# Moving work between engines in the first scan of a fused SSD and GELU kernel

## The chip, the cores and the metric

The kernel runs on one core of one Trainium2 chip. The time is device time in microseconds (us) of one launch, given as the median of several runs. All arithmetic on matrices is in fp32; in the records a fp32 matmul appears as two records.

## What is computed

Two layers, one behind the other. The first is a state space scan in chunks over 4 batches, 8 heads and 768 positions, with head width 32 and state width 16:

```python
L = np.exp(cum[:, :, :, None] - cum[:, :, None, :]) * causal
CB = np.einsum('bhin,bhjn->bhij', Cc, Bc)
y_intra = np.einsum('bhij,bhjd->bhid', CB * L, xc)
y_inter = np.einsum('bhin,bhnd->bhid', Cc, state) * np.exp(cum)[:, :, :, None]
y[:, :, sl] = y_intra + y_inter
state = decay_full * state + np.sum(Bx, axis=2)
```

`cum` is the running sum of `log(a)` inside a chunk. The result, 3072 tokens by 256, goes through a feed-forward layer with 2048 hidden columns:

```python
h = x @ w_in
g = h * (1.0 / (1.0 + np.exp(-1.702 * h)))
out = g @ w_out
```

The weights and the output differ in type: the weights come as float64 and are unpacked on the chip into fp32.

## The kernel before

The 3072 tokens are worked on in six groups of 512 (`NG = 6`, `TG = 512`). A group is two pairs of 128-token chunks (`PG = 2`). Scan chunks are 64 positions long (`H = 64`), so that a group holds eight of them. For each group the scan yields `yT`, its transposed output, and the feed-forward layer then computes 16 blocks `h` of 128 hidden columns each and the products with `w_out`. Groups 0 and 1 do the start of the feed-forward layer with plain matmuls (`hidden`, L889); group 0's products are plain too (`project_all`, L987); the rest uses a scheme with seven products (`first`, L945 and L955; `product`, L1050 and L1057).

The order of the work on each engine is the order in which the code issues it, and it is fixed at the end (`in_order`): no scheduler changes it. Each engine works through its own queue; waits between engines are semaphores that follow from the tiles. SyncE's queue issues nearly all transfers, in order too.

The change touches the first scan, group 0, both pairs p = 0 and 1, which is written out by hand in L1165 to L1212. Its steps:

- `keep_busy` and `pads` (L435, L428): matmuls on ones whose result nobody uses. `pads(9, busy)` at L1171 stands ahead of the last of eight masks (`mask`, L548), which lay -1e5 above the diagonal into PSUM.
- `turn_first` (L612): VectorE transposes C and B in 32x32 blocks as soon as they have landed.
- `differ_of` (L1153, matmuls L554) and `decay_exp` (L570, ScalarE L575): the decay matrix L = exp(difference of `cum`) for both pairs.
- `mask_first` (L644): C for each pair is spread into two copies `CT`, one for each of the Q = 2 heads that share 32 partitions, each multiplied by the column `part[:, q]`, which is 1 on that head's rows and 0 elsewhere. GpSimd does both pairs (L650). For pair 1 a one-element memset by VectorE (L649) holds it back.
- `fields` (L188): VectorE splits the upper words of a piece of weights into exponent and mantissa (L192, L195). `clamp` (L198, ScalarE L203, L204), `rounded` (L206, VectorE L208) and `join` (L215, VectorE L222 and L228) make fp32 of it. Piece i of `PIECES` holds some of the 16 column blocks: piece 0 blocks 0 and 1, piece 1 blocks 2 and 3, piece 2 blocks 4 and 5.
- `turn_back` (L622, L627): TensorE transposes B back. `ends_first` (L465, VectorE L468): B times the decay to the end of the chunk, `Be`.
- `score` (L669, matmuls L682): the products of C and B. Both pairs' results lie in one tile of PSUM. Between the two pairs `since_first` is called (L506): two matmuls of rows (L512) and two exponentials by ScalarE (L517) that give `since`, the decay since the start of a chunk.
- `weigh` (L688, VectorE L693): L times the scores, pair by pair. `fetch(1, held=True)` (L163) writes one element by VectorE (L171) between the two; the transfer of piece 1, and all transfers behind it on SyncE's queue, wait for it.
- `drops` (L520): ScalarE spreads the decay of each chunk over 64 columns for the scan (L522, 448 elements in each partition).
- `gain` (L701, matmuls L713): the increments of the state, `A`, in two banks. `parts_first` (L726, L730): ScalarE copies them into `steps`, so that the eight chunks of a column lie side by side.
- `since_start` (L661, L667), on GpSimd here: `CsT`, C times `since`.
- `keep_first` (L732): one VectorE scan over `drop` and `steps` (L735) gives the states of all eight chunks. The states are then copied for each pair into `state[p]`, half of each by ScalarE (L743) and half by VectorE (L744), each half multiplied by its column of `part`.
- `dense(2)` (L1157, L1161): two further matmuls of ones.
- `finish` (L788): on TensorE the parts inside the chunks (`intra`, L833), then the parts from the states (`inter`, L821), and ScalarE's copies into `yT` (L850). Then `hidden(0, f)` begins.

`hidden(1, f)` splits its first matmuls by columns: the first two (f = 0) in four pieces of 128 columns, the next three in two pieces of 256.

## Time and profile before

| | us |
|---|---|
| three runs | 350.84, 352.07, 352.6 |
| median | 352.07 |
| the profiled execution | 349.68 |
| its span, first to last instruction | 347.8 |
| TensorE busy in the span | 342.0 (98%) |
| VectorE busy | 253.5 (73%) |
| ScalarE busy | 153.1 (44%) |
| GpSimd busy | 12.9 (4%) |

The granted TensorE clock is 1.000 over the span. A profile lists instructions with the line of the code that issued them, the tile that they write and the tiles that they read. In a timeline a row gives the start, the time from the start of the first to the end of the last instruction of the row, engine, line, operation, operands, shapes and count; in square brackets stands idle time of that engine ahead of it and what ended it ("issue" where the profile shows nothing that was waited for). PE is TensorE, PEld its weight loads, DVE VectorE, ACT ScalarE, POOL GpSimd, and SPq SyncE's queue of transfers. Instructions of one engine overlap by some hundredths of a microsecond, and a matmul's end is modelled, so starts are compared with starts.

### The profile page before, as it was taken

Reading aid. Unit: us, or ns where it says so; the run is one execution under the profiler, and the core shown is the slowest. Engines: PE = TensorE matmul, PEld = TensorE weight load, DVE = VectorE, ACT = ScalarE, POOL = GpSimd, SP = SyncE. Lnnn points to the kernel's source line nnn. Section 1 sums busy time; section 2 is a strip of 40 time slices with the busy share of each in tenths; the row PEclk is TensorE's granted clock in tenths of the full one; section 3 lists DMA queues with packets and bytes.
Section 4 is the critical chain, followed back from the end, with each engine's and each line's share of the span. In section 5 each row is a group of like instructions: output and inputs, shape, how many; then the busy total and the mean of one; then the engine's idle time right before and its main releaser. Section 6 shows DMA issues by size and latency. Waiting matters only on the chain.

```text
span 347.8 us, 8141 instructions
## 1 busy us (share of the span) xinstructions
PE 342.0 (98%) x3392; PEld 271.9 (78%) x3392; DVE 253.5 (73%) x479; ACT 153.1 (44%) x349; POOL 12.9 (4%) x41
## 2 busy tenths in 40 slices
PE   8899999999999999999999999999999999999996
PEld 6644444557788888888888888888888888899996
DVE  5899999998679998839995649787555654455463
ACT  5698573107354324744332543442444321554320
POOL 8300000000000100000000000000000000000000
PEclk9999999999999999999999999999999999999999
DMA  6699997435526100435613036300000300000301
GB/s 162 142 336 193 283 212 155 81 77 93 105 58 128 33 2 15 63 104 102 101 28 50 2 81 117 64 2 1 2 2 2 61 2 0 0 2 0 62 0 61
DMA packets 89980, 25.92 MB, mean 75 GB/s; under 512 B 73432, under 2 KB 87128, under 8 KB 89944
## 3 DMA queue, kind: packets, MB, share of 16 engines
q1 hardware_dynamic: 89112, 24.88, 33.3%
q10 hardware_dynamic: 832, 0.52, 0.5%
q8 instruction: 26, 0.43, 0.5%
q14 instruction: 10, 0.08, 0.1%
HBM read 22.15 MB, written 3.24 MB: 73 GB/s over the span
## 4 chain that ended last, share of the span: by engine, by line
PE 97%; ACT 1%; DVE 1%; issue 0%; DVEq 0%
PE acc L1050 28%; PE X L945 20%; PE Y L955 14%; PE h L889 10%; PE o L987 8%; PE acc L1057 7%; PE y L833 2%; PE y L821 2%; PE cb L682 2%; PE A L713 1%; PE busy L440 1%; PE ab L554 1%; PE ab L548 0%; DVE steps L735 0%; ACT steps L730 0%; ACT drop L522 0%
## 5 line engine op out<-in xcount | busy, mean ns | idle before, releaser
L950 ACT ACTIVATE ac<-X 128x256 f32<-128x256 f32 x76 | 29.1, 383 | 78.6 <-PE X L945 78.2
L1050 PE MATMUL acc<-mg,mw 128*128 128x256 f32 x192 | 54.5, 379 | 0.0
L922 ACT ACTIVATE gT<-gT 128x512 f32<-128x512 f32 (+1 forms) x76 | 39.3, 520 | 34.1 <-DVE gT L1077 33.4
L1077 DVE TENSOR_TENSOR gT<-Y,ac 128x512 f32<-128x512 f32 x38 | 26.2, 689 | 36.1 <-PE Y L955 30.5
L945 PE MATMUL X<-my,mi 128*128 128x256 f32 x152 | 45.2, 380 | 0.0
L1077 DVE TENSOR_TENSOR gT<-Y,b 128x256 f32<-128x256 f32 x38 | 15.8, 419 | 35.2 <-PE Y L955 35.2
L1050 PEld LDWEIGHTS acc<-mg,mw 128*128 128x128 f32 x192 | 36.5, 190 | 5.0
L1050 PE MATMUL acc<-gT,w_out 128*128 128x256 f32 x128 | 35.5, 379 | 0.0
L889 PE MATMUL h<-yT,w_in 128*128 128x512 f32 (+2 forms) x98 | 35.5, 518 | 0.0
L945 PEld LDWEIGHTS X<-my,mi 128*128 128x128 f32 x152 | 28.0, 190 | 4.1 <-ACT ac L950 0.4
L889 PEld LDWEIGHTS h<-yT,w_in 128*128 128x128 f32 x98 | 17.0, 190 | 16.5 <-issue 14.3
L987 PE MATMUL o<-gT,w_out 128*128 128x512 f32 x64 | 28.6, 597 | 0.0
L913 DVE TENSOR_TENSOR mg<-gT 128x512 f32<-128x512 f32 x40 | 27.2, 681 | 0.0
L1050 PEld LDWEIGHTS acc<-gT,w_out 128*128 128x128 f32 x128 | 24.2, 190 | 3.4 <-ACT yT L860 0.2
L950 ACT ACTIVATE b<-X 128x256 f32<-128x256 f32 x38 | 14.6, 384 | 20.0 <-PE X L945 19.6
L945 PE MATMUL X<-yT,w_in 128*128 128x256 f32 x76 | 23.2, 389 | 0.0
L945 PE MATMUL X<-my,w_in 128*128 128x256 f32 x76 | 22.7, 382 | 0.2 <-issue 0.2
L955 PE MATMUL Y<-yT,w_in 128*128 128x256 f32 x76 | 22.7, 381 | 0.0
L955 PE MATMUL Y<-my,mi 128*128 128x256 f32 x76 | 22.6, 379 | 0.0
L955 PE MATMUL Y<-yT,mi 128*128 128x256 f32 x76 | 22.5, 379 | 0.0
L987 PEld LDWEIGHTS o<-gT,w_out 128*128 128x128 f32 x64 | 11.8, 190 | 13.2 <-issue 12.7
L402 DVE TENSOR_TENSOR_SCAN L<-a,idents 128x1024 f32<-128x1024 f32 x9 | 20.5, 2277 | 0.4 <-DMA a<-scratch 0.4
(156 smaller groups left out, 544.2 us busy)
## 6 DMA issues: line engine op xcount, KB each, us to landing
a<-scratch SPq DMA_DIRECT2D x18, 256.0 KB, 5.3
bits<-in_moe_w_out_dram SPq DMA_DIRECT2D x8, 512.0 KB, 5.4
x<-in_x_dram SPq DMA_DIRECT2D x24, 128.0 KB, 3.0
out_dram<-ob SPq DMA_DIRECT2D x40, 64.0 KB, 1.9
bits<-in_moe_w_in_dram SPq DMA_DIRECT2D x8, 256.0 KB, 4.6
bits<-in_moe_w_in_dram SPq DMA_DIRECT2D x4, 512.0 KB, 9.3
b<-in_B_dram SPq DMA_DIRECT2D x20, 64.0 KB, 3.0
af<-in_a_dram SPq DMA_DIRECT2D x3, 384.0 KB
```

What stands on the lines that cost most here:

```text
L402: nc.vector.tensor_tensor_scan(out=L, data0=ra[p].rearrange("p k e -> p (k e)"), data1=idents.rearrange("p h i -> p (h i)"), initial=0.0, ...
L682: nc.tensor.matmul(out=s["cb"][side, r, k].rearrange("p (q i) -> p q i", q=Q), lhsT=BT[rows, k, side], rhs=CT[rows, k, :, side], start=Tru ...
L889: nc.tensor.matmul(out=h[:, cols], lhsT=w_in[:, f, k], rhs=yT[g][:, k, cols], start=(k == 0 and e == 0), stop=(k == NK - 1), skip_group_ch ...
L913: nc.vector.tensor_tensor(out=t[:, 0:2], in0=B[:, :, 1], in1=B[:, 0], op=ALU.subtract)
L922: nc.scalar.activation(o, i, AF.Silu, scale=GELU_SCALE)
L945: nc.tensor.matmul(out=s["X"], lhsT=lhsT, rhs=rhs, start=i == "1", stop=i == "4", skip_group_check=True)
L950: nc.scalar.activation(copy, s["X"], AF.Copy)
L955: nc.tensor.matmul(out=o, lhsT=lhsT, rhs=rhs, start=s.pop("new", False), stop=i != "5", skip_group_check=True)
L987: nc.tensor.matmul(out=o[c], lhsT=w_out[:, c, f], rhs=gT[g, f // 2][:, f % 2], start=(f == 0), stop=(f == NF - 1), skip_group_check=True)
L1050: nc.tensor.matmul(out=acc[g][0][i][:, cols], lhsT=w, rhs=h[:, cols], start=(j == 0 and k == 0 and (i, 0) in begins), stop=(j == NF // 2 - ...
L1057: nc.tensor.matmul(out=o[k] if type(o) is list else o[:, cols], lhsT=h[:, cols], rhs=w, start=(j == 0 and (i, k) in begins), stop=(j == NF ...
L1077: nc.vector.tensor_tensor(out=o, in0=v, in1=w, op=ALU.add)
```

## The change

In the first scan:

- C's mask for pair 1 is made by VectorE, in two steps with `part[:, q]` as scalar, instead of by GpSimd; the one-element memset goes. It is issued ahead of `fields(0)`.
- `since_first`, `drops` and both `since_start` are called behind `turn_back` and ahead of `ends_first` and of both pairs' scores. The rows' matmuls so come ahead of both scores on TensorE.
- `drops` is a GpSimd copy instead of a ScalarE copy.
- `clamp(0)` comes behind the scores, on ScalarE's queue now ahead of `parts_first`.
- `parts_first` multiplies by `part` when it copies the increments, in four instructions instead of two, so that the scan runs over masked increments; `keep_first` then copies each pair's states plainly, pair 0 by VectorE and pair 1 by ScalarE, each in one instruction.
- `rounded(0)` comes behind `keep_first`, so on VectorE's queue behind the scan and the copy.
- 15 fillers instead of 9 stand ahead of the last mask, which are 12 more records; and `hidden(1, f)` splits its first three matmuls in two pieces and no other.

```diff
     def drops():
-        nc.scalar.copy(
+        nc.gpsimd.tensor_copy(
             drop[:, :, 1:], since[0][:, :CG].rearrange("p c (s i) -> p (c s) i", s=2)[:, 1:, H - 1].unsqueeze(
                 1).to_broadcast([P, Q * D, 2 * CG - 1]))
...
         if p:
-            nc.vector.memset(s["CT"][:, 0, 0, :1], 0.0)
+            for q in range(Q):
+                nc.vector.tensor_scalar(out=s["CT"][:, :, q], in0=s["tp"], scalar1=part[:, q:q + 1],
+                                        scalar2=None, op0=ALU.mult)
+            return
         nc.gpsimd.tensor_tensor(
...
     def parts_first():
-        to = steps.rearrange("p e (c s) -> p s c e", s=2)
+        to = steps.rearrange("p (q d) (c s) -> p s q c d", s=2, q=Q)
         for i in range(2):
-            nc.scalar.activation(to[:, i], increment[0][i], AF.Copy)
+            o = increment[0][i].rearrange("p c (q d) -> p q c d", q=Q)
+            for q in range(Q):
+                nc.scalar.activation(to[:, i, q], o[:, q], AF.Copy, scale=part[:, q:q + 1])
...
-        o = steps.rearrange("p (q d) m -> p q m d", q=Q)
-        for p in range(PG):
+        for p, copy in zip(range(PG), (nc.vector.tensor_copy, nc.scalar.copy)):
             state[p] = ssd.tile([P, 4, Q * D], FP32, tag="S", name=f"S{p}", bufs=3)
-            to = state[p].rearrange("p m (q d) -> p q m d", q=Q)
-            m = slice(4 * p, 4 * p + 4)
-            nc.scalar.activation(to[:, 0], o[:, 0, m], AF.Copy, scale=part[:, 0:1])
-            nc.vector.tensor_scalar(out=to[:, 1], in0=o[:, 1, m], scalar1=part[:, 1:2], scalar2=None,
-                                    op0=ALU.mult)
+            copy(state[p], steps.rearrange("p e m -> p m e")[:, 4 * p:4 * p + 4])
...
-            n = 2 if g == 1 and NK * f + k < 5 else 1
-            if n == 2 and NK * f + k < 2:
-                n = 4
+            n = 2 if g == 1 and NK * f + k < 3 else 1
...
-            pads(9, busy)
+            pads(15, busy)
...
     fields(0)
-    mask_first(1)
     turn_back()
+    since_first()
+    drops()
+    for p in range(PG):
+        since_start(p, nc.gpsimd)
     ends_first(0)
     ends_first(1)
-    score(range(PG), since_first)
+    score(range(PG))
+    clamp(0)
     weigh(0)
     fetch(1, held=True)
...
-    rounded(0)
-    drops()
     gain(range(PG))
     parts_first()
-    for p in range(PG):
-        since_start(p, nc.gpsimd)
-    clamp(0)
     keep_first()
+    rounded(0)
     dense(2)
```

`mask_first(1)` moves to just ahead of `fields(0)`.

More of the change, by code (lines that the diff above doesn't have):

```diff
@@ L1180 @@
         decay_exp(1, r, ab[1, r])
+    mask_first(1)
     fields(0)
-    mask_first(1)
     turn_back()
+    since_first()
+    drops()
+    for p in range(PG):
+        since_start(p, nc.gpsimd)
     ends_first(0)
     ends_first(1)
-    score(range(PG), since_first)
+    score(range(PG))
+    clamp(0)
     weigh(0)
```

## The prediction

> **What bounds the kernel now.** I read the busy times first, then the chain of work that ended last, then the timelines of the first 24 us engine by engine, and at last the transfers of that stretch. The busy table and the chain say that TensorE is the bound nearly everywhere:

> ```profile
> PE 342.0 (98%) x3392; PEld 271.9 (78%) x3392; DVE 253.5 (73%) x479; ACT 153.1 (44%) x349; POOL 12.9 (4%) x41
> ```

> The change lies almost wholly in the first 18 us, where the chain is not TensorE's alone. It runs through the fillers (L432), the masks (L548, L554), the transposes, scores and rows, then ScalarE and VectorE, and back to TensorE at the first L821 matmul. On VectorE and ScalarE (start, length, engine, line):

> ```profile
> 11.36 2.36 DVE L693 TENSOR_TENSOR L<-L,cb 128x1024 f32<-128x1024 f32 x2 [1.12 <-PE cb L682]
> ...
> 13.64 0.69 DVE L208 SCALAR_TENSOR_TENSOR m<-bits,m 128x512 f32<-128x512 uint32 x1
> 14.24 1.22 DVE L735 TENSOR_TENSOR_SCAN steps<-drop,steps 128x512 f32<-128x512 f32 x1
> 15.49 0.58 DVE L744 TENSOR_SCALAR S<-steps,part 128x128 f32<-128x128 f32 x2
> 15.99 0.42 DVE L222 SCALAR_TENSOR_TENSOR p<-bits,p 128x256 uint32<-128x256 uint32 x1
> ```

> ```profile
> 10.66 0.66 ACT L517 ACTIVATE since<-rows 128x256 f32<-128x256 f32 x2 [1.17 <-PE rows L512]
> 11.35 1.01 ACT L522 COPY drop<-since 128x448 f32<-128x448 f32 x1
> 12.27 1.11 ACT L730 ACTIVATE steps<-A 128x256 f32<-128x256 f32 x2
> ```

> The scan L735 waits for nothing on its own account at 14.24: ScalarE's L730 ended at 13.38, but L208 (an unpacking step of the weights) stands ahead of it on VectorE until 14.3. TensorE then waits for the scan's states, and afterwards streams:

> ```profile
> 16.12 1.68 PE L821 MATMUL y<-CsT,S 32*64 32x64 f32 x56 [0.70 <-DVE S L744]
> 17.78 17.53 PE L889 MATMUL h<-yT,w_in 128*128 128x512 f32 x40
> ```

> The 40 records look unbroken, but the weight loads beneath them show a second limit:

> ```profile
> 20.46 0.19 PEld L889 LDWEIGHTS h<-yT,w_in 128*128 128x128 f32 x1 [0.24 <-issue]
> ...
> 20.50 0.69 DVE L228 SCALAR_TENSOR_TENSOR w_in<-m,p 128x512 f32<-128x512 f32 x1
> ...
> 21.31 0.30 PEld L889 LDWEIGHTS h<-yT,w_in 128*128 128x128 f32 x2 [0.66 <-issue]
> ```

> Every weight load comes 0.24 after the one before ended; the one at 21.31 comes 0.66 after. It is the first of h2 (third column block), whose weights VectorE finishes at 20.50 + 0.69 = 21.19. So **h2 already starts when VectorE lets it**, about 0.1 us late, whatever TensorE did before. VectorE in turn has no hole from 13.64 to 21.19, and its unpacking of pieces 1 and 2 meets their transfers:

> ```profile
> bits<-in_moe_w_in_dram SPq DMA_DIRECT2D x2, 256.0 KB, 3.7
> ```

> These two (piece 1) are issued at 12.63 and 13.04 behind a held memset that follows the first L693. In the trace's landing events the second half of piece 1 lands at 17.59 and VectorE reads it at 17.69; piece 2 lands at 18.98 and is read at 19.10. The DMA share in 16 to 20 us is 0.95.

> **The change, part by part.**

> *Fillers* (9 to 15 matmuls, 18 to 30 records). The 18 records take 0.37 us and the mask behind them starts 0.44 after their start; groups of four start about 0.03 apart. Twelve more are three groups, +0.1 us (bounds 0 and 12/18 of 0.44 = 0.29). VectorE's cumulative scan ends at 5.48 and L554 starts at 5.64 straight behind the mask, so nothing hides this.

> *Rows ahead of both scores.* Transposes, scores, rows, scores start at 8.72, 9.31, 9.93, 10.56, A at 11.18: each group costs 0.62 with its change of tile shape. Inside a score group the steps are 0.06 to 0.11; to the next group about 0.20. With the two scores adjacent one change goes: -0.1 us (bounds 0 and -0.14). It pays for the fillers, so the second score's end and L693 stay at 11.36. The rows need ScalarE's L575 (8.94 and 9.22 in the trace), and run from about 9.4, so L517 ends near 10.8 instead of 11.32.

> *C's second mask on VectorE.* GpSimd's 1.04 us (9.44 to 10.48) goes; two 128x256 tensor-by-scalar steps come to VectorE, 0.29 each by L341, with 0.55 as upper end (L192, 128x512). Fields and Be move back by 0.5 to 1.1, into VectorE's 1.12 us of idle ahead of L693; Be is then ready by 10.8 at the latest, and A wants it at 11.18. Cost: nothing; without this hole it would be 0.5. A row against it: L192 took 0.55 beside GpSimd's mask at 8.46 and 0.43 alone at 17.69, so they disturb each other. [...]

> *Drops on GpSimd.* ScalarE loses 1.01 us. GpSimd shows no such copy: 128x512 products cost 1.03, so 448 elements 0.9 as lower end; a 128x12 strided copy (L485) costs 0.205 against 0.098 for a one-element memset, 9.7 ns an element, 4.4 as upper end. I take 1.2, nearest to the products: 10.8 to 12.0. The two CsT products (1.43) follow to 13.5, wanted at 15.5. The scan wants the drops at 13.7, so cover is 1.7 us. [...]

> *Clamp ahead of the parts, parts in four.* ScalarE: L517 to 10.8, clamp 1.4 to 12.2, then A, which ended for L730 at about 12.2 and does not move (its last quarter waits for x). Four 128x128 steps with a scale replace two 128x256 of 1.11 together. Bounds on start to start: 0.20 (L767, 128x64 from PSUM, eight in 1.70) and 0.43 (L743, 128x128, strided); I take 0.3, near L767, as both read PSUM. The last ends at 12.27 + 0.9 + 0.4 = 13.6 (12.27 + 0.6 + 0.33 = 13.2 to 12.27 + 1.3 + 0.5 = 14.1). VectorE is in L693 until 13.7. So cover holds, or 0.4 is lost.

> *Scan, copies, rounding.* With L208 behind it, the scan starts at 13.64, not 14.24: **-0.60**. State copies at 14.90: VectorE 128x256, 0.42 (L468 form) to 0.66 (two L744), I take 0.47 as L744's stride remains; ScalarE about 0.75 (two of L743 less one start), for pair 1 alone, which L821 reaches 0.4 later. L821 starts at about 15.5 instead of 16.12, and the last L833 ends at 15.42, so TensorE can follow. h0 would start 0.6 earlier.

> *What is late next.* On VectorE the sum is: scan 13.64, copy 14.90, L208 15.28, first L222 at 15.88 instead of 15.99: -0.11, since the work is only reordered (0.58 of L744 for one copy). Then piece 1's landing, 17.59, holds L192 at 17.65, and piece 2's 18.98 holds the next L192 at 19.08. The held memset has not moved, so these landings have not. join(1) ends at 21.15 and h2 starts 0.02 to 0.05 earlier than now. **Of TensorE's 0.6 us, 0.55 become a wait in front of h2.** From h4 on (weights at 24.08, wanted at 24.85) there is room again, so the shift at h2 is the shift of all that follows.

> *hidden(1).* 4-way and 2-way splits become 2-way and none: sixteen 128-column records at 0.112 become eight at 0.216 (1.79 against 1.73), the rest costs the same: -0.06. Behind this point TensorE has issued as many matmuls as before.

> **Sum.** -0.04 - 0.06 = -0.1 us. The profiled execution took 349.68 (span 347.8 and 1.9 around it), so 349.6; the median of the three runs shown, 352.07, lies 2.4 above it; against that I forecast **352.0**.

> **Rivals.**
> 1. *The gain goes through*: the landings come earlier or VectorE's copy is cheap, and h2 follows: -0.6 - 0.06, 351.4. For it: L192 at 17.69 also follows its predecessor closely. Against: VectorE itself gains only 0.11, and two landings stand in the way.
> 2. *Slower: the drops on GpSimd end the wait.* It decides from 13.64 - 10.8 = 2.8 us on. At 4.4 us the scan starts at 15.2, L222 at 17.5, h2 1.5 later: 353.5. Against: all larger GpSimd rows are under 3 ns an element; for: the 128x12 copy.
> 3. *The parts do not get short*: 0.43 apart, scan at 14.1, VectorE +0.35, h2 +0.35: 352.4. The change then does not free the scan.
> 4. *Pauses or clock*: TensorE's own 0.42 pause at 14.69 ("issue") moves with the fillers, or the 0.55 wait lowers its clock. At the start the 192-column matmuls come 0.32 apart until 3.9, against 0.216 for 256 columns later; that is half speed, so 3 us of it again would cost 1.5, and with the pause 1.9: 353.9. Against: the 0.70 wait at 16.12 was followed by full speed.

> **Numbers.** Forecast 0.55, rival 1 0.15, rival 2 0.12, rival 3 0.12, rival 4 0.06. From 351.4 to 353.5 all but rival 4 are inside; the runs shown spread from 350.84 to 352.6, so I widen the low end to 350.9. Within 0.5% (1.8 us, about what a measurement of this kernel can tell from no change): all but rival 4 and the spread of runs. Faster 0.06, same 0.84, slower 0.10.

> **What would show it.** Right: scan near 13.7, L821 near 15.5, L889's first start near 17.2, and a hole of about 0.5 before h2's weights at 21.3. Wrong: h2 before 21.0 (rival 1), scan released by GpSimd (2) or by ScalarE after 13.9 (3), granted clock under 1 or a long issue pause (4). The forecast fails if landings of pieces 1 and 2 move.

## The result and the profile after

The changed kernel takes 352.88 us (350.89 to 355.01), beside 351.26 (349.70 to 353.27) for the kernel before on the same chip; the ratio is 1.0041, 95% interval 1.0026 to 1.0056. So it is **slower by 0.4%**, about 1.4 us, where the forecast was a tenth of a microsecond gained. The time lies between the 350.9 and the 353.5 of the prediction, but it moved the other way.

The profiled execution took 351.12, with a span of 349.3. The one that the prediction was made from, 349.68, is shorter than every one of the 22 executions of the kernel before in the comparison. The two profiles differ by 1.4 and the medians by 1.6, but each profile is a single execution; which of their differences belong to the change is for the experiments.

The busy table of the changed kernel's page:

```profile
PE 342.4 (98%) x3392; PEld 271.6 (78%) x3392; DVE 253.9 (73%) x479; ACT 152.2 (44%) x349; POOL 12.8 (4%) x41
```

As many matmuls and weight loads as before. VectorE of the changed kernel (timeline: start, length, engine, line; the idle time ahead in brackets):

```profile
11.92 2.36 DVE L696 TENSOR_TENSOR L<-L,cb 128x1024 f32<-128x1024 f32 x2 [0.96 <-PE cb L685]
13.09 0.06 DVE L171 MEMSET bits<- 128x1 uint32 x1
14.20 1.22 DVE L740 TENSOR_TENSOR_SCAN steps<-drop,steps 128x512 f32<-128x512 f32 x1
15.45 0.40 DVE L745 COPY S<-steps 128x256 f32<-128x256 f32 x1
15.77 0.68 DVE L208 SCALAR_TENSOR_TENSOR m<-bits,m 128x512 f32<-128x512 uint32 x1
...
19.87 0.43 DVE L192 TENSOR_SCALAR p<-bits 128x512 uint32<-128x512 uint32 x1 [0.43 <-DMA bits<-in_moe_w_in_dram]
...
21.27 0.69 DVE L228 SCALAR_TENSOR_TENSOR w_in<-m,p 128x512 f32<-128x512 f32 x1
```

The scan now follows L696 (the old L693) directly, 2.28 behind its start; before it was 2.88. That is the 0.60 that was forecast. But L696 itself starts 0.56 late, at 11.92, so the scan stands at 14.20, and the held memset at 13.09 is late as well. Piece 2 lands at 19.77 (18.98 before), VectorE waits 0.43 for it, and the weights of h2 are ready at 21.96 (21.19). ScalarE of the changed kernel:

```profile
11.30 0.73 ACT L203 ACTIVATE p<-p,edge 128x512 f32<-128x512 uint32 x1
12.06 0.72 ACT L204 ACTIVATE p<-p,edge 128x512 uint32<-128x512 f32 x1
12.74 1.27 ACT L735 ACTIVATE steps<-A,part 128x128 f32<-128x128 f32 x4
15.45 0.68 ACT L745 COPY S<-steps 128x256 f32<-128x256 f32 x1 [1.44 <-DVE steps L740]
```

The clamp and the four parts end at 14.01, just in time. TensorE of the changed kernel:

```profile
15.26 0.84 PE L833 MATMUL y<-L,x 64*32 64x64 f32 x62 [0.46 <-issue]
16.03 1.68 PE L821 MATMUL y<-CsT,S 32*64 32x64 f32 x56
17.70 3.70 PE L887 MATMUL h<-yT,w_in 128*128 128x512 f32 x8
22.27 1.98 PE L887 MATMUL h<-yT,w_in 128*128 128x512 f32 x4 [0.87 <-DVE w_in L228]
```

The states no longer hold TensorE: L821 follows L833 without a gap. What the scan gained is waited for in front of h2, 0.87, as "what is late next" said. h2 starts at 22.27, where before it was 21.34.

Following the same matmul through both traces gives the shift of the changed kernel: +0.93 at h2, +0.81 behind hidden(1), +1.1 behind 117 us, +1.5 behind 260 us, and +1.46 at the end. So 0.65 us comes at 117 us and later, some 30 us and more behind the last matmul that the change touched (in hidden(1), at 86 us). The timeline of TensorE at 259 us, first of the kernel before:

```profile
258.66 0.59 PE L955 MATMUL Y<-yT,w_in 128*128 128x256 f32 x2
259.42 0.70 PE L945 MATMUL X<-my,w_in 128*128 128x256 f32 x2 [0.16 <-issue]
```

and of the changed kernel:

```profile
259.37 0.59 PE L953 MATMUL Y<-my,mi 128*128 128x256 f32 x2
260.55 0.59 PE L953 MATMUL Y<-yT,w_in 128*128 128x256 f32 x2 [0.59 <-issue]
```

Both pause once, waiting for nothing that a semaphore shows ("issue"); the changed kernel one product earlier in the program, and longer by 0.43, which is the spacing of the products here.

### The profile page after: what moved, and what is told of

The parts are those of the page before. It is cut to its first block, busy times and chain, and to the rows that moved or that the text cites. A ratio compares the mean times of both kernels' runs of the same rounds, so it can differ in the third digit from the quotient of the medians.

```text
span 349.3 us, 8144 instructions
## 1 busy us (share of the span) xinstructions
PE 342.4 (98%) x3392; PEld 271.6 (78%) x3392; DVE 253.9 (73%) x479; ACT 152.2 (44%) x349; POOL 12.8 (4%) x41
## 4 chain that ended last, share of the span: by engine, by line
PE 95%; DMA 1%; DVE 1%; issue 1%; SPq 0%; ACT 0%; DVEq 0%
PE acc L1048 28%; PE X L943 19%; PE Y L953 14%; PE h L887 9%; PE o L985 8%; PE acc L1055 7%; PE y L833 2%; PE cb L685 2%; PE y L821 1%; DMA bits<-in_moe_w_in_dram 1%; PE A L716 1%; PE busy L440 1%; PE ab L554 1%; PE ab L548 1%; SPq L180 0%
## 5 line engine op out<-in xcount | busy, mean ns | idle before, releaser
L887 PE MATMUL h<-yT,w_in 128*128 128x512 f32 (+1 forms) x86 | 35.6, 568 | 0.9 <-DVE w_in L228 0.9
L887 PEld LDWEIGHTS h<-yT,w_in 128*128 128x128 f32 x86 | 16.0, 190 | 18.1 <-issue 14.1
L402 DVE TENSOR_TENSOR_SCAN L<-a,idents 128x1024 f32<-128x1024 f32 x9 | 20.5, 2277 | 0.7 <-DMA a<-scratch 0.7
## 6 DMA issues: line engine op xcount, KB each, us to landing
a<-scratch SPq DMA_DIRECT2D x18, 256.0 KB, 5.6
bits<-in_moe_w_in_dram SPq DMA_DIRECT2D x8, 256.0 KB, 4.3
```

The costliest lines, as they stand in the source:

```text
L402: nc.vector.tensor_tensor_scan(out=L, data0=ra[p].rearrange("p k e -> p (k e)"), data1=idents.rearrange("p h i -> p (h i)"), initial=0.0, ...
L887: nc.tensor.matmul(out=h[:, cols], lhsT=w_in[:, f, k], rhs=yT[g][:, k, cols], start=(k == 0 and e == 0), stop=(k == NK - 1), skip_group_ch ...
```

## The experiments

Three theories; the third, hinted at in the expectation of e2, was framed only when e1's profile was there. **Front**: the six fillers delay the masks, and the held memset hands that on to the landings and to h2 (with the clock as a part of it: full clock granted later). **Rest**: the moved rows, masks, parts and copies cost. **Place**: the twelve records shift where each later instruction of TensorE stands in its stream, and with that the places where TensorE pauses. Ratios are to the kernel before on the same chip, with 95% intervals.

### The parts alone

e1_more_fillers: the kernel before with the six fillers.

```diff
-            pads(9, busy)
+            pads(15, busy)
```

> The kernel before with 15 fillers in place of 9, nothing else. Clock theory (in the profile of after TensorE reached its full clock at 5.7 us instead of 4.4, because the longer stretch of small fillers makes the first microseconds look less busy, in some executions by a whole step of 2 to 3 us): +1.0 to +1.6 us in the median and two groups of times about 2.5 us apart. Landing theory (the front is late by 0.1 to 0.2, the held memset hands this to the transfers of pieces 1 and 2, join and h2): +0.1 to +0.3 us, one group. Rest theory (the loss comes from the moved rows, masks and copies): 0 to +0.1.

1.0043 (1.0016 to 1.0070), 1.5 us between the medians. The fillers alone cost as much as the whole change. The times are what the clock theory of this expectation (the clock part of front) gave, two groups too: four of twelve at 355.07 to 355.82, the rest at 351.71 to 353.29. The profiled execution, 355.07, is of the longer group. Why the clock should come late, that small fillers make the start look less busy and that it moves by a whole step, is that theory's guess and no run shows it. Its full clock comes at 6.46 and its h2 at 23.38, 2.04 later than in the kernel before, but 3.4 us more are lost behind h4, where that theory has nothing to say. Of its profile, TensorE:

```profile
258.38 1.44 PE L833 MATMUL y<-L,x 64*32 64x64 f32 x122
261.61 0.31 PE L833 MATMUL y<-L,x 64*32 64x64 f32 x6 [1.79 <-issue]
...
262.38 0.98 PE L955 MATMUL Y<-my,mi 128*128 128x256 f32 x2
263.15 1.06 PE L955 MATMUL Y<-yT,w_in 128*128 128x256 f32 x2
```

The pause has grown to 1.79 and stands earlier in the program, among the small matmuls of y; behind it two products take 0.98 to 1.06 instead of 0.59, for the granted clock is one half from 262.46 to 265.88.

e2_fewer_splits: the kernel before with the new splits of hidden(1), six matmuls fewer.

```diff
-            n = 2 if g == 1 and NK * f + k < 5 else 1
-            if n == 2 and NK * f + k < 2:
-                n = 4
+            n = 2 if g == 1 and NK * f + k < 3 else 1
```

> The kernel before with the first three matmuls of hidden(1) in two pieces and no other, nothing else. Clock theory, landing theory and rest theory: -0.06 us, no measurable change. If instead the position of later matmuls in TensorE's stream of instructions counts (12 records fewer from here on), +0.5 us or more.

0.9990 (0.9975 to 1.0005), no pause near 259 us. The splits are worth what was forecast or nothing, and the 0.5 us that a shift of the later matmuls was to cost here does not show.

e3_rest_alone: the changed kernel with 9 fillers and the old splits.

```diff
-            pads(15, busy)
+            pads(9, busy)
...
-            n = 2 if g == 1 and NK * f + k < 3 else 1
+            n = 2 if g == 1 and NK * f + k < 5 else 1
+            if n == 2 and NK * f + k < 2:
+                n = 4
```

> The changed kernel with 9 fillers and with the old splits of hidden(1), so all of the change but its records. Clock theory: within 0.3 us of before, one group of times. Landing theory: -0.1 to +0.1. Rest theory: +1.2 to +1.6, as the whole change.

1.0006 (0.9983 to 1.0029): no gain and no loss is to be seen, where the rest theory expected 1.2 to 1.6 us of loss, so that theory falls. Its profile has a pause of 0.77 near 261 us all the same.

e5_both_records: the kernel before with fillers and splits, so that as many matmuls as before stand ahead of everything from the end of hidden(1) on.

```diff
-            pads(9, busy)
+            pads(15, busy)
...
-            n = 2 if g == 1 and NK * f + k < 5 else 1
-            if n == 2 and NK * f + k < 2:
-                n = 4
+            n = 2 if g == 1 and NK * f + k < 3 else 1
```

> The kernel before with 15 fillers and with the new splits of hidden(1), so the records of the change without its rest: later matmuls stand at the same place in TensorE's stream as before. Clock theory (more small fillers delay the full clock): +1.2 to +1.6 us, as with 15 fillers alone. Place theory (with 15 fillers alone, the loss came from a pause of 2.0 us in the L833 group at 260 us, in which TensorE has nothing to issue, and from half clock for 3.4 us behind it, because the stream stood 12 records further on): +0.1 to +0.3 us.

1.0016 (0.9984 to 1.0048): between the theories, it decides nothing.

### The held memset

e4_early_hold: the changed kernel with the hold ahead of both L696.

```diff
+    fetch(1, held=True)
     weigh(0)
-    fetch(1, held=True)
```

> The changed kernel with the held memset ahead of the first weighing, so that piece 1 and what is behind it is issued about 1.2 us earlier. Landing theory: pieces 1 and 2 land 1 us earlier, h2 follows TensorE, 0.6 to 0.9 us faster than the changed kernel. Clock theory: 0.5 us or less faster than the changed kernel, two groups of times remain. Rest theory: no better than the changed kernel by more than 0.3.

1.0030 (1.0006 to 1.0055): no gain. Piece 2 landed at 17.84 rather than 19.77, but h2 started at 22.67, no earlier: TensorE's pause in L833 grew from 0.46 to 1.5 us, to 16.38. The transfer of TensorE's instructions ahead of this pause began at 14.08 instead of 12.97, when the weights' transfers were already issued, and took 0.95 us as before. That the one delayed the other is not shown: without the early hold the same pause was 0.74 in e6 and 0.94 in e13.

### The number of fillers

e6_14_fillers and e7_9_fillers: the changed kernel with 14 and with 9. e8_after_again: the changed kernel unaltered, on their chip.

```diff
-            pads(15, busy)
+            pads(14, busy)
```

```diff
-            pads(15, busy)
+            pads(9, busy)
```

> The changed kernel with 14 fillers in place of 15, so two records fewer ahead of everything. The changed kernel has three waits more in TensorE's stream than before, and its pause at 259.6 us is 0.59 against 0.16. Place theory: the pause goes back to 0.2 or less, 0.3 to 0.5 us faster than the changed kernel. Clock theory: 0.1 us or less.

> The changed kernel with 9 fillers and its own, new splits, so 12 records fewer ahead of everything. Place theory: no pause at 259 us, as with the new splits alone on the kernel before, and 0.3 to 0.5 us faster than before. Clock theory: as the rest of the change alone, within 0.3 us of before. Rest theory: 1 us or more slower than before.

> The changed kernel once more, unaltered, for a second profile and for its spread in the same call: a median 1.2 to 1.6 us above before, with times near 351.1 and others near 353.5 to 354.3. Clock theory: a slow profile has its full clock 2 us or more later than a quick one. Place theory: a slow profile has a longer pause without cause in a group of small matmuls, and perhaps half clock behind it.

1.0003 (0.9980 to 1.0026) with 14; 0.9990 (0.9969 to 1.0011) with 9; 1.0019 (0.9998 to 1.0040) with 15. Pauses near 260 us in the three profiles: 0.3 (place expected 0.2 or less), none, 0.9. Fillers cost: by medians the changed kernel takes 1.2 us more than with 9 on this chip. And the cost does not show in the first 20 us: with 9 fillers h2 started at 22.57, as late as in the changed kernel (22.27 and, in e8, 22.49).

### Place against front

What separates the two is a fixed count. I number TensorE's instructions in each trace from the first (matmul records, weight loads and waits; a filler matmul counts four), and take from the DMA records when each transfer of TensorE's instructions began; all of these move 16,384 bytes (26 on queue 8 in the profiles of before and after, 0.43 MB). The gap is from the start of the instruction before the count to the one at it; without a pause it is about 0.2 among products and under 0.05 among the small ones. The idle times in brackets are shorter, as they begin at the modelled end of the matmul before. "Shift" is how many counts the later instructions stand behind the kernel before.

| kernel | shift | gap at 704 | at 960 | at 1728 | at 3520 | at 5824 |
|---|---|---|---|---|---|---|
| before | 0 | 0.64 | - | - | - | 0.54 |
| changed | +3 | 0.67 | - | - | - | 0.96 |
| e1, 6 more fillers | +24 | 0.42 | - | - | - | 2.00 |
| e9, six late | +4 | 0.80 | - | - | - | 1.36 |
| e10, twelve late | +28 | - | 2.11 | - | - | 1.91 |
| e7, 9 fillers | -21 | 0.82 | - | - | - | - |
| e11, 9 fillers | -21 | 0.29 | - | 0.78 | - | - |
| e13, six taken out behind | -21 | 1.15 | - | - | - | - |
| e14, 3 fillers | -45 | 0.37 | - | - | 1.09 | - |

In all twenty profiles the pauses that TensorE makes for no semaphore stand at counts 704 + 256 k, whichever matmul stands there, and they end 2.2 to 2.9 us after the transfer of instructions ahead of them began. I take the transfers in order, one to each count from 448 on. Where the profiles of before and after have a pause, TensorE had come to the count 1.4 to 1.9 us after its transfer began; at all the other counts, without a pause, it came 2.5 us or more after. So my reading is that TensorE pauses where it comes to such a count too soon after its transfer began; the traces show the times, not what happens between the end of the transfer and the end of the pause. It comes there soon where small matmuls stand ahead: in the kernel before 2.35 us pass from count 5568, most of it L833, to the last instruction ahead of the pause at 5824, and 25.32 from 6080 to 6336, all of it products. For count 5824 the transfer begins at 257 to 262 us, in the kernel before and the changed one while TensorE is in the small matmuls of y; count 5824 lies some products behind them, and each product that lies between takes 0.43 off the pause. The change added no matmul there but three waits (52 for 49 in TensorE's stream), which bring the count forward by one product: 0.16 becomes 0.59. Six fillers without fewer splits (e1) bring it right into the small matmuls: 1.79. Six matmuls fewer than in the changed kernel move it out behind six more products, and the pause is gone. The other profiles agree: the gap is 0.54 and 0.70 in the two where the count stands in the same product as before (the kernel before and e6), 0.86 to 1.42 in the ten where it stands one product earlier, 1.91 and 2.00 in the two where it stands in small matmuls, and there is none in the six with a shift of -21 or below. TensorE of e11, the changed kernel with 9 fillers, at the same place:

```profile
260.18 0.59 PE L953 MATMUL Y<-my,mi 128*128 128x256 f32 x2
260.61 0.59 PE L953 MATMUL Y<-yT,w_in 128*128 128x256 f32 x2
```

At most counts of this row nothing is to be seen; at one to three in a profile TensorE stood idle for 0.15 to 1.9 us.

e9_six_late and e10_twelve_late put six and twelve fillers into TensorE's wait for the scan instead.

```diff
-            pads(15, busy)
+            pads(9, busy)
...
             t = bank("dense")
+            pads(6, t)
```

```diff
-            pads(15, busy)
+            pads(9, busy)
...
             t = bank("dense")
+            pads(12, t)
```

e11_nine_again and e12_after_third are the kernel with 9 fillers (edit of e7) and the changed kernel, on their chip.

> The changed kernel with 9 fillers ahead of the last mask, and the six others issued with the two matmuls of ones behind A, where TensorE waits for the scan. From that point on every instruction of TensorE has the same place in its stream as in the changed kernel, while the masks and the exponentials run as with 9 fillers. Front theory (the fillers cost because they delay the masks and, through the held memset, the landings of pieces 1 and 2): like the kernel with 9 fillers, ratio 0.997 to 1.000 against the kernel before. Place theory (the twelve records move the points at which TensorE's instructions are fetched, and a pause there costs the time): like the changed kernel, ratio 1.002 to 1.004, with a pause of 0.5 us or more near 259 us.

> As the one before, with twelve fillers in place of six in that late position: TensorE's later instructions stand 12 records further on than in the changed kernel. Place theory: as the kernel before with six more fillers, which stood 12 records on as well and took 1.0043, so 1.003 to 1.006, with a pause of more than 1 us near 259 us. Front theory: 0.997 to 1.001, for the fillers lie in TensorE's wait for the scan.

> The changed kernel with 9 fillers, a second time, on the chip of the other three. It took 0.999 (0.9969 to 1.0011) the first time. Front and place theory: 0.997 to 1.000, and no pause near 259 us. If the first time was luck of the chip: 1.002, as the changed kernel.

> The changed kernel unaltered, beside the three others: both theories 1.002 to 1.004. Place theory: a pause near 259 us of 0.5 us or more in its profile. Front theory: full clock granted later than 5 us and the landing of piece 2 later than 19.5.

e9 0.9995 (0.9973 to 1.0017), e10 **1.0114** (1.0070 to 1.0159), e11 0.9958 (0.9934 to 0.9982), e12 1.0021 (0.9993 to 1.0050). e10 is what front can't give, for its masks run as with 9 fillers, though place expected less of it, 1.003 to 1.006; TensorE in its profile:

```profile
17.70 1.74 PE L821 MATMUL y<-CsT,S 32*64 32x64 f32 x53
21.33 0.43 PE L821 MATMUL y<-CsT,S 32*64 32x64 f32 x3 [1.89 <-issue]
```

Count 960 has come into the small matmuls of the first inter group, count 5824 into those at 264 us (1.70), and the granted clock is one half from 14.60 to 18.01 and from 21.43 to 24.84 in this execution. Not all of the 1.0114 need be place, then: the first of the two half-speed stretches follows a wait of A for Be, 1.3. e9 lies between e11 and e12. By its ratio to the kernel before it is what front expected (0.997 to 1.000) and not place (1.002 to 1.004), though it has the pause (1.0). But both theories also said what it is to be like. Front said: like 9 fillers. On its chip e9's median, 351.62, is 1.2 us above that of 9 fillers, 350.45 (e11); drawing again and again at random from the two sets of twelve times gives a ratio of medians of 1.0033, 95% interval 1.0014 to 1.0051. Place said: like the changed kernel, which is at 352.46 (e12), 1.0024 (0.9993 to 1.0056) above e9: not resolved, so that a part of up to some 2 us may still be front.

e13_fillers_front_rest_out keeps the front and takes the place back. e14_three_fillers moves it on by another 24 counts; e15_nine_third is the kernel with 9 fillers (edit of e7) on their chip.

```diff
-            pads(15, busy)
+            pads(14, busy)
...
-            n = 2 if g == 1 and NK * f + k < 3 else 1
+            n = 1
...
-    dense(2)
+    dense(0)
```

```diff
-            pads(15, busy)
+            pads(3, busy)
```

> The changed kernel with 14 fillers in front, without the two matmuls of ones behind A and without any split in hidden(1). That takes out six matmuls, so that from hidden(1) on each of TensorE's instructions has the place that it has in the kernel with 9 fillers, while the front has five of the six fillers. Place theory: like the kernel with 9 fillers, ratio 0.996 to 1.000, no pause near 259 us (the missing splits may cost up to 0.2 us in front of hidden(1)). Front theory: like the changed kernel, 1.001 to 1.004.

> The changed kernel with 3 fillers instead of 15: another twelve records less than with 9. Front theory: no slower than with 9 fillers, 0.995 to 0.999, as the masks come some 0.2 us earlier. Place theory: no pause at the count 5824, which lies later in the products of X and Y still; what the other boundaries meet decides: count 960 falls deeper into group 0's h, count 1728 into other parts of the scan of a later group; 0.994 to 1.002, and if it is slower than with 9 fillers a pause at one of the counts 704 + 256 k shows where.

> The changed kernel with 9 fillers, a third time: 0.996 to 0.999 by both theories.

e13 0.9982 (0.9961 to 1.0004): with 14 fillers in front it is as fast as with 9, e15's 0.9988 (0.9972 to 1.0004), as place expected and front did not (1.001 to 1.004). e14 **1.0036** (1.0017 to 1.0054): fewer fillers than any, and as slow as the changed kernel. Front expected 0.995 to 0.999 of e14, place 0.994 to 1.002: place says where pauses stand, but it did not foresee what they cost. The pause in e14's profile is at a count where no other kernel pauses, 3520, now among small matmuls:

```profile
149.88 0.97 PE L833 MATMUL y<-L,x 64*32 64x64 f32 x73
151.73 0.78 PE L833 MATMUL y<-L,x 64*32 64x64 f32 x55 [0.88 <-issue]
```

That execution took 350.71 and is the shortest of e14's twelve (median 352.44), so what a usual one loses is not seen; from h4 to the last matmul it takes 320.5 us, e15's 319.3.

So 3, 9 and 15 fillers give 1.0036, 0.9979 (mean of three) and 1.0027 (mean of three): not a line, as a delay would be, but a matter of what stands at those counts. What the front adds is not resolved: e13 against e15 says nothing, -0.0006, and e12 against e9 0.0026, with some 0.003 and 0.004 to each side.

### The spread

e16_after_look_1, e17_after_look_2, e18_after_look_3: the changed kernel unaltered, to see what its longer executions do.

> The changed kernel, one profiled execution. Each execution has a chance of about a half to lie above 352.4. If it does: place theory, the sum of TensorE's pauses at the counts 704, 960, 1728 and 5824 is larger by 1 us or more than in the profile of 351.12, whose pauses there are 0.45 and 0.6; front theory, the start of h2 is later by 1 us or more (22.27 there) and the stretch behind it is as long as there. If it lies below 352: both as in the profile of 351.12.

> A second look at the unaltered changed kernel. Above 352.4: larger pauses at the counts 704, 960, 1728 or 5824 by 1 us or more (place theory), or h2 later than 23.3 with an unchanged stretch behind it (front theory). Below 352: both as in the profile of 351.12.

> A third look at the unaltered changed kernel. Above 352.4: larger pauses at the counts 704, 960, 1728 or 5824 by 1 us or more (place theory), or h2 later than 23.3 with an unchanged stretch behind it (front theory). Below 352: both as in the profile of 351.12.

352.70, 352.71 and 351.48. The two long ones differ. In e16 piece 2 lands 8.23 us after piece 1 was issued (6.57 in the changed kernel's first profile), h2 starts at 23.61, and the rest is as there: a landing, as front expected of a long execution. In e17 h2 starts at 22.74, and the pauses are larger: 1.04 at 5824 (0.59), 0.20 at 1728, where there was none, and 0.53 at 704 (0.46): 0.7 more together, less than the 1 us that place expected; 0.65 of it lies behind h4, where the stretch to the end is 1.1 longer. From h4 to the last matmul the six profiles of the changed kernel take 320.3 to 321.5 (mean 320.6), the three with 9 fillers and e13 319.2 to 320.2 (mean 319.5). That 1.1 us stands behind h4, where the masks and the first pieces of weights are long done; between the medians of the same two kernels it was 1.2 on one chip and 2.0 on the other. What an execution of 354 or 355 does was not caught.

## Why the prediction was wrong, step by step

- **Fillers, +0.1** (bounds 0 and 0.29): the step that failed. It counted only the delay of the masks. Measured, the fillers cost 1.5 us alone (e1), and the changed kernel takes 1.2 and 2.0 us more with 15 than with 9, by medians. The delay of the masks costs nothing that e13 could show, within some 0.9 us. What the twelve records do besides is move every later instruction by 24 counts, and with that what stands under TensorE's pauses; the sum had no term for it.
- **"Behind this point TensorE has issued as many matmuls as before"**: true (3392 and 3392) and taken for the end of the matter; this is the same step. The fillers and the fewer splits cancel; three more waits, which nobody counts as work, do not, and the pause at 259 us went from 0.16 to 0.59. With 9 fillers the shift is -21, and the pause is gone. I had seen the pause at 14.69 in the profile and named "pauses or clock" as rival 4, at 0.06, but priced it only there, and asked neither what decides where it stands nor whether there were others. The direction is that rival's; its price, 1.9 at the first scan, is not.
- **h2 starts 0.02 to 0.05 earlier**: it started 0.93 later in the profile. "The held memset has not moved" was wrong for this execution, as the masks ran later (full clock granted from 5.75, before from 4.37). Neither can be given to the change: without the fillers, or with them, full clock came between 4.06 and 7.37 in the profiles that show it. h2 started at 21.34 to 23.38 in the kernel before and its variants e1, e2 and e5, and at 22.27 to 23.61 in six executions of the changed one. I had one execution, a short one, and took its times for the kernel's. Whether the moved work delays h2 stays open: with it h2 started at 21.74 or later in every profile, without it at 21.34, 21.48, 22.00 and 23.38, and four are too few to tell.
- **Scan 0.60 earlier, and swallowed in front of h2**: right in the first profile of the changed kernel, where it is 2.28 from L696's start to the scan's, and in e17 (2.30). In the four others of the changed kernel, e8, e12, e16 and e18, it is 2.66 to 3.42, where the last x lands late, A ends late and with it ScalarE's parts. The scan of e8:

```profile
14.71 1.23 DVE L740 TENSOR_TENSOR_SCAN steps<-drop,steps 128x512 f32<-128x512 f32 x1 [1.05 <-ACT steps L735]
```

  That is rival 3's place, by another cause.
- **Drops on GpSimd 1.2**: 0.99, from 11.48; the two CsT end at 13.86. Rival 2 falls.
- **Parts in four**: 0.25 to 0.29 apart (forecast 0.3), ending at 14.01 (forecast 13.6, bounds 13.2 to 14.1).
- **C's mask on VectorE, at nothing**: it fits the hole, 0.96 of idle time is left ahead of L696. One of its two steps took 0.77 beside GpSimd's product, above the upper end of 0.55; the other, alone, 0.34.
- **State copies**: VectorE 0.40 (forecast 0.47), ScalarE 0.68 (0.75).
- **hidden(1), -0.06**: the shift falls by 0.12 there. Right in sign, but twice the size forecast.

The 1.46 between the two profiles is so: 0.93 at h2, which lies within the spread between executions and can't be given to the change; -0.12 in hidden(1); 0.31 at 117 us, where X waits for ScalarE's `ac`; 0.34 at 259 us, which is place (0.43 of idle time, of which 0.10 is won back in the next product). At 117 us ScalarE waits for VectorE, and VectorE's scan L402 had waited for the transfer `a<-scratch`, first of the kernel before, then of the changed kernel, with TensorE's wait below:

```profile
106.87 2.29 DVE L402 TENSOR_TENSOR_SCAN L<-a,idents 128x1024 f32<-128x1024 f32 x1 [0.37 <-DMA a<-scratch]
```

```profile
108.00 2.29 DVE L402 TENSOR_TENSOR_SCAN L<-a,idents 128x1024 f32<-128x1024 f32 x1 [0.71 <-DMA a<-scratch]
...
118.59 0.48 PE L943 MATMUL X<-my,mi 128*128 128x256 f32 x1 [0.31 <-ACT ac L948]
```

TensorE's wait stands, 0.16 to 0.35 long, in all six profiles of the changed kernel and in those of e3, e4, e5, e6, e9 and e10, and in none of the kernel before, e1, e2, e7, e11, e13, e14 and e15. So it goes with the shift, too, but not in a way that place explains; why the transfer lands later stays open.

So the profiles put a name to 0.65 us of the loss behind h2. That the fillers cause the loss is shown by e1 and by taking them out; that most of it is place and not front rests on e10, e13 and e14, and on e9 beside e11. Its size in a usual execution is not accounted for in full.

The version that the experiments point to is the changed kernel with 9 fillers: 0.9990, 0.9958 and 0.9988, below the kernel before all three times, though only the second interval excludes 1. It is faster than the changed kernel on the two chips that had both: drawn as above, the changed kernel takes 1.0033 (1.0012 to 1.0054) and 1.0058 (1.0023 to 1.0092) of its time.

## What to carry over

When a change adds or removes instructions on the engine that sets the time, even fillers and waits, count what stands ahead of every later "issue" pause: in all twenty profiles here the pauses stayed at counts 704 + 256 k, and other work moved under them. Test such an edit with its count made good elsewhere (e13) before a difference under 1% is put down to the edit itself. And take a short step of the front from several profiles, for its times moved here by more than the change did.
